# Half-height tiles of TensorE for the block-diagonal products of a fused attention and FFN kernel, and twelve weight pieces split on TensorE

## The chip, the cores and the metric

The kernel runs on one core of a Trainium2 chip. The metric is the device time of one execution in microseconds. The kernel before took 1536.48 us (median of 3 runs, 1536.45 to 1540.12).

## The reference, cut to what matters

Three stages follow each other on 8 batches of 576 tokens with 8 heads of 64 (512 features).

```python
# 1. attention through 32 landmarks (means of 18 tokens)
A, Bm, C = sm(q, k_lm), sm(q_lm, k_lm), sm(q_lm, k)
Z = Bm.T / (norms);  six times: Z = 2 * Z - Z @ Bm @ Z
x = A @ Z @ C @ v                                   # [B, 576, 512] after joining the heads
# 2. Fourier mixing and an FFN of 2048
u = x + real(fft(fft(x, axis=1), axis=2))
un = (u - mean(u)) / sqrt(var(u) + 1e-6)
x = u + relu(un @ w_ch1) @ w_ch2
# 3. a gated FFN of 1024 on token-shifted inputs
k = relu(xk @ w_k);  out = sigmoid(xr @ w_r) * ((k * k) @ w_v)
```

## The kernel before, in words

The 4608 tokens are cut into 9 blocks of 512. Stage 1 and the Fourier part work on one batch at a time, the two FFNs on one block at a time. The large products run in float16 with each operand split into a high and a low half (three products of 128x512 instead of one): 1728 for w_ch1 (named `ph`), 1728 for w_ch2 (`acc`) and 2160 for stage 3. All small products of stage 1 and of the Fourier part are float32 and named `gp`; the profile shows each of those as two MATMUL records, and a transpose as one.

The order is not that of the code. `Plan` records every operation with an estimated cost, then schedules all engines by priority (`Plan.issue`) and issues the instructions of each engine in that order; each engine then works strictly in it. Where the plan believes TensorE idle it adds fillers (`warm`, L1043): products of zeros, into a spare PSUM bank before the first FFN product (`spare<-zero`), later into the open accumulator (`acc<-zero`).

What the change touches, by name and line:

- `Weights.run` (L538): an FFN weight piece of 128x512 arrives in 8-byte words; ACT and DVE make float32 of it (`wst` or `more`), ACT writes the high half (`w1h`, `w2h`), and DVE computes the low half as 64 w - high (`w1l`, `w2l`, L574). Pieces come in the order in which block 0 needs them.
- `series` (L806): after six steps of the inverse, Y (32 landmarks x 64 features for each head, four heads of a group g in 128 partitions) is written as a block diagonal `bdY` of 128x256.
- `tail` (L894): four transposes of `bdY` give `YT`; four products with the table `cs`, each in half of the array's columns (128x64), give the feature side of the Fourier transform (`YC`, `YS`); `mixed(j)` gives the token side of 128 features in `d1`, `d2`, and `xu(t, ...)` multiplies a quarter of the block diagonal by `AT` and adds it to `d1` and `d2` as the next block's input `ub`. There are four `xu` for each batch, each with one product of 289 and one of 288 columns, over all 128 rows of which two heads' rows are zero. The Nyquist row (`psN`, `yn`) is one row of 289 columns.
- `norm(i)` (L1111): for blocks 0 and 1 the mean over features is taken by four products with `ones` and the variance by sixteen one-column products; blocks 2 to 8 add on POOL and DVE first and need one product and four transposes.

```python
for i in range(NB):
    while nb < B and S * nb < BLK * (i + 1):
        batch(nb)
        nb += 1
    block_a(i, norm(i))
```

So block 0 needs batch 0, block 1 needs batch 1, and the other batches are put in between the FFN products of earlier blocks.

Of the kernel before, what the change touches and what calls it, by code (L numbers as in the profile page):

```python
# [11 lines left out]
F32 = mybir.dt.float32  # L12
# [10 lines left out]
M = 32  # L23
# [14 lines left out]
def slot_features():  # L38
    f = np.arange(DM)
    f[257:] = 512 - np.arange(1, 256)  # L40
    return f
# [151 lines left out]
class Plan:  # L193
# [328 lines left out]
class Weights:  # L522
# [15 lines left out]
    def run(self, src, hi, lo, room=None):  # L538
# [35 lines left out]
        v_.scalar_tensor_tensor(lo, w, WS, hi, op0=ALU.mult, op1=ALU.subtract)  # L574
# [4 lines left out]
def phase1(a, iss, psum, const, pool, ident, ublock):  # L579
# [4 lines left out]
    def tile(shape, name, tag=None, bufs=1):  # L584
        return iss.tile(pool, shape, F32, name, tag, bufs)
# [30 lines left out]
    mask4 = load_const("mask4", [128, 4])  # L616
    eye32 = load_const("eye32", [128, M])
# [41 lines left out]
    def chain_a(b):  # L659
# [3 lines left out]
        A = [tile([97, 2, 256], f"A{c}") for c in range(3)]  # L663
# [78 lines left out]
    def chain_b(b):  # L742
# [8 lines left out]
        BB = tile([128, 2, 2, M], "BB")  # L751
# [54 lines left out]
        def series():  # L806
            for i in range(6):
                for g in range(2):
                    ps = psum()[0]
                    w = M + D if i < 5 else D  # L810
                    mm(ps[:, 0:w], flat(bdR[g]), RX[g][:, M + D - w:], True, True)
                    if i < 5:
                        v_.tensor_tensor(bdR[g], spread4(ps[:, 0:M]), m41, op=ALU.mult)
                        s_.activation(RX[g][:, 0:M], ps[:, 0:M], AF.Copy)
                    v_.tensor_tensor(RX[g][:, M:], ps[:, w - D:w], RX[g][:, M:], op=ALU.add)

            bdY = T["bdY", b] = tile([128, 2, 260], "bdY")
            psY = psum()[0]
            for g in range(2):
                mm(psY[:, D * g:D * g + D], flat(bdB[:, g]), RX[g][:, M:], True, True)  # L820
            for g in range(2):
                v_.scalar_tensor_tensor(
                    bdY[:, g, g:g + 256].rearrange("p (h d) -> p h d", d=D),
                    psY[:, D * g:D * g + D].unsqueeze(1).to_broadcast([128, 4, D]),
                    rc[:, g:g + 1], mask4.unsqueeze(2).to_broadcast([128, 4, D]),
                    op0=ALU.mult, op1=ALU.mult,
                )
            g_.tensor_copy(bdY[:, 1, 0:1], bdY[:, 1, 256:257])
# [65 lines left out]
    def tail(b):  # L894
# [9 lines left out]
        YT = tile([128, 2, 2, 64], "YT", "t1")  # L904
        pT = psT.rearrange("p (g x) -> p g x", g=2)
        s_.activation(YT[:, :, 0], pT[:, :, 0:64], AF.Copy)
        s_.activation(YT[:, :, 1], pT[:, :, 192:256], AF.Copy)
# [6 lines left out]
        for g in range(2):  # L914
            ps = psum()[0]
            for hp in range(2):
                mm(
                    ps[64 * hp:64 * hp + 64, :], YT[:, g, hp, :], cs[:, 2 * g + hp, :],
                    True, True,
                )  # L920
            s_.activation(YC[:, g], ps[:, 0:256], AF.Copy)
            s_.activation(YS[:, g, 1:256], ps[:, 257:512], AF.Copy)
            s_.activation(yn[:, g:g + 1], ps[:, 256:257], AF.Copy)
# [3 lines left out]
        def mixed(j):  # L927
# [9 lines left out]
            d1 = tile([128, HS], "d1")  # L937
            d2 = tile([128, HS], "d2")
# [6 lines left out]
            return d1, d2  # L945

        def xu(t, da, db):
            g = t // 2
            pa, pb = psum()[0], psum()[0]
# [4 lines left out]
            for i, lo, hi in cuts(base, base + HS):  # L954
                v_.tensor_tensor(
                    ublock(i)[t][:, lo - BLK * i:hi - BLK * i],
                    pa[:, lo - base:hi - base], da[:, lo - base:hi - base], op=ALU.add,
                )
            end = base + S
            for i, lo, hi in cuts(base + HS, end):  # L960
                l, h = lo - BLK * i, hi - BLK * i
                v_.tensor_tensor(
                    ublock(i)[t][:, h - 1:(l - 1 if l else None):-1],
                    pb[:, end - hi + 1:end - lo + 1], db[:, end - hi + 1:end - lo + 1],
                    op=ALU.add,
                )

        d1, d2 = mixed(0)
        xu(0, d1, d2)
        psN = psum()[0]  # L970
        for g in range(2):
            mm(psN[0:1, 0:HS], yn[:, g:g + 1], AC[:, g], g == 0, g == 1)
        s_.activation(d1[0:1, :], psN[0:1, 0:HS], AF.Copy)
        s_.activation(d2[0:1, :], psN[0:1, 0:HS], AF.Copy)
        xu(2, d2, d1)
        d1, d2 = mixed(1)
        xu(1, d1, d2)
        xu(3, d2, d1)

# [11 lines left out]
def build(nc, tc, a):  # L991
# [5 lines left out]
    with stack, tc.manual_schedule():  # L997
# [50 lines left out]
        iss.warm = warm  # L1048
        w1 = [iss.tile(pa, [128, 4, FF1], F16, f"w1{x}") for x in "hl"]
# [61 lines left out]
        def norm(i):  # L1111
# [4 lines left out]
            if i < 2:  # L1116
# [10 lines left out]
            if i < 2:  # L1127
# [104 lines left out]
        for n, x in enumerate(w12_items):  # L1232
            weights.run(*x, room=rooms[n % 3] if n < 24 else None)
# [169 lines left out]
def consts():  # L1403
    mask2 = np.zeros((128, 2), np.float32)
    mask4 = np.zeros((128, 4), np.float32)
    for p in range(128):
        mask2[p, p // 64] = 1.0 / 18
        mask4[p, p // 32] = 1.0
    eye32 = np.tile(np.eye(M, dtype=np.float32), (4, 1))
# [15 lines left out]
    for i in range(4):  # L1425
        for p in range(128):
            f = 128 * i + p if i < 2 else 511 - (128 * (i - 2) + p)
            ang = 2 * np.pi * ((f * kk) % DM) / DM
            cs[p, i, 0:257] = np.cos(ang)
            cs[p, i, 257:512] = np.sin(ang[1:256])  # L1430
    return dict(
        mask2=mask2, mask4=mask4, eye32=eye32, bones=bones,
# [49 lines left out]
```

## Time and profile before

| | |
|---|---|
| median of the runs | 1536.48 us |
| the profiled execution, whole | 1536.68 us |
| its span, first to last instruction | 1534.9 us |
| TensorE busy | 1522.2 us (99%) |
| VectorE busy | 818.0 us (53%) |
| ScalarE busy | 578.2 us (38%) |
| GpSimd busy | 287.2 us (19%) |
| mean granted TensorE clock | 0.998 |
| first FFN product starts | 77.34 us |

An engine's busy time counts a record from its start to its modelled end; on TensorE records overlap, so the pace is read from the starts, not from the lengths. The interval from one start to the next is what an instruction costs that engine.

### The profile page before, as it was taken

What the parts mean: (1) busy time and instruction counts of PE and PEld (TensorE: products, weight loads), DVE (VectorE), ACT (ScalarE), POOL (GpSimd) and SP (SyncE); (2) the same over time, 40 slices, a digit from 0 to 9 for tenths busy, and PEclk for the clock granted to TensorE, in tenths of its full rate; (3) what the DMA queues carried; (4) which work ended last, traced back from release to release, by engine and by line L of the source; (5) the groups of instructions that cost most, each with busy time, mean ns of one, the idle gap of its engine ahead of it and who ended that gap; (6) DMA issues with size and microseconds to landing.
All of it is one profiled execution on the core that took longest, in us unless ns stands there. A gap on an engine that the chain in (4) does not pass through costs nothing.

```text
span 1534.9 us, 20950 instructions
## 1 busy us (share of the span) xinstructions
PE 1522.2 (99%) x8284; PEld 777.8 (51%) x8284; DVE 818.0 (53%) x1698; ACT 578.2 (38%) x1181; POOL 287.2 (19%) x351
## 2 busy tenths in 40 slices
PE   9999999999999999999999999999999999999998
PEld 5655555555645645645544444444444444444443
DVE  7888667667636426426135171212777765653222
ACT  4667464445413213213212131113655544443221
POOL 3021103113102102102002040001544432231100
PEclk9999999999999999999999999999999999999999
DMA  8434252433301001000004000002011101000000
GB/s 290 159 125 153 79 179 73 144 122 123 101 35 63 32 28 62 2 28 1 1 28 165 1 28 1 28 0 83 28 56 55 55 28 55 28 13 16 28 28 28
DMA packets 43586, 97.86 MB, mean 64 GB/s; under 512 B 4064, under 2 KB 9440, under 8 KB 42976
## 3 DMA queue, kind: packets, MB, share of 16 engines
q1 hardware_dynamic: 43488, 96.53, 18.4%
q8 instruction: 65, 1.06, 0.3%
q14 instruction: 33, 0.27, 0.1%
HBM read 72.39 MB, written 24.12 MB: 63 GB/s over the span
## 4 chain that ended last, share of the span: by engine, by line
PE 96%; DMA 1%; DVE 1%; ACT 1%; issue 0%; SPq 0%; POOL 0%; ACTq 0%; DVEq 0%
PE ph L330 37%; PE acc L330 36%; PE gp L330 21%; PE gp L346 2%; DMA ident<-in_ident 1%; DMA wst<-in_w_ch 0%; DVE small L186 0%; PE spare L1043 0%; SPq L315 0%; DVE uc L186 0%; DMA out<-o 0%; DVE d L186 0%; ACT d L186 0%; ACT wtop L186 0%; DVE o L186 0%
## 5 line engine op out<-in xcount | busy, mean ns | idle before, releaser
L330 PE MATMUL ph<-un,w1h 128*128 128x512 f16 x1152 | 349.9, 379 | 0.4 <-DVE uc L186 0.3
L330 PE MATMUL acc<-h,w2h 128*128 128x512 f16 x1152 | 348.5, 379 | 0.0
L186 DVE SCALAR_TENSOR_TENSOR h<-ph,h 128x512 f16<-128x512 f32 x144 | 99.2, 689 | 302.6 <-ACT h L186 302.2
L186 ACT ACTIVATE h<-ph 128x512 f16<-128x512 f32 x144 | 85.9, 596 | 390.7 <-PE ph L330 390.4
L330 PE MATMUL ph<-un,w1l 128*128 128x512 f16 x576 | 218.6, 380 | 0.0
L330 PE MATMUL acc<-h,w2l 128*128 128x512 f16 x576 | 218.3, 379 | 0.1
L330 PE MATMUL ph<-xk,w_k 128*128 128x512 f16 x864 | 199.6, 379 | 0.0
L330 PE MATMUL acc<-w_v,k 128*128 128x512 f16 x864 | 198.9, 379 | 0.0
L330 PEld LDWEIGHTS <-w2h 128*128 128x128 f16 x1152 | 113.0, 99 | 128.4 <-issue 5.7
L330 PEld LDWEIGHTS <-w1h 128*128 128x128 f16 x1152 | 112.7, 99 | 127.8 <-issue 7.4
L330 PEld LDWEIGHTS <-k 128*128 128x128 f16 x864 | 84.5, 98 | 100.6
L330 PEld LDWEIGHTS <-w_k 128*128 128x128 f16 x864 | 84.5, 98 | 99.7
L186 DVE TENSOR_TENSOR rk<-rk 128x512 f32<-128x512 f32 x72 | 55.5, 770 | 146.3 <-ACT rk L186 145.9
L330 PE MATMUL gp<-w_r,xr 128*128 128x512 f16 x432 | 99.3, 379 | 0.7 <-ACT rs L186 0.7
L186 ACT ACTIVATE rk<-ph 128x512 f32<-128x512 f32 x72 | 42.9, 596 | 129.2 <-PE ph L330 121.6
L330 PEld LDWEIGHTS <-w1l 128*128 128x128 f16 x576 | 57.1, 99 | 65.1 <-issue 4.4
L330 PEld LDWEIGHTS <-w2l 128*128 128x128 f16 x576 | 56.7, 98 | 63.2 <-issue 0.6
L186 DVE TENSOR_TENSOR k<-rk,k 128x512 f16<-128x512 f32 x72 | 59.3, 823 | 29.2 <-ACT k L186 29.0
L186 POOL TENSOR_TENSOR sq<-sq 128x513 f32<-128x513 f32 x27 | 36.7, 1360 | 198.6 <-ACT sq L186 198.1
L186 POOL TENSOR_TENSOR xr<-xt,xr 128x512 f16<-128x512 f32 x36 | 48.6, 1374 | 112.1 <-ACT xr L186 112.0
L330 PEld LDWEIGHTS <-xr 128*128 128x128 f16 x432 | 42.3, 98 | 51.4 <-issue 0.9
L186 DVE TENSOR_TENSOR xt<-xt,rs 128x512 f32<-128x512 f32 x72 | 60.5, 869 | 2.9 <-ACT rs L186 2.8
(162 smaller groups left out, 1919.1 us busy)
## 6 DMA issues: line engine op xcount, KB each, us to landing
wst<-in_w_ch SPq DMA_DIRECT2D x24, 512.0 KB, 3.9
q<-in_q SPq DMA_DIRECT2D x16, 578.0 KB, 5.1
k<-in_k SPq DMA_DIRECT2D x16, 576.0 KB, 4.9
ys<-ub SPq DMA_DIRECT2D x36, 256.0 KB, 2.1
out<-o SPq DMA_DIRECT2D x36, 256.0 KB, 2.1
yb<-ys SPq DMA_DIRECT2D x8, 1026.0 KB, 5.1
v<-in_v SPq DMA_DIRECT2D x8, 1024.0 KB, 5.9
more<-in_w_ch SPq DMA_DIRECT2D x8, 512.0 KB, 4.6
```

The source lines that it names most:

```text
L186: f(real(out), *map(real, args), **{k: real(x) for k, x in kw.items()})
L330: self.nc.tensor.matmul(out.real(), lhsT=lhsT.real(), rhs=rhs.real(), start=start, stop=stop, **kw)
L346: self.nc.tensor.transpose(out.real(), in_.real(), ident.real())
```

## The change

Four things are done.

1. `bdY` holds only two heads side by side (128x128 for a group, was 128x256): rows 0 to 63 are one pair of heads, rows 64 to 127 the other. `xu(g, ...)` issues two products over 64 rows each, into two banks, instead of two over 128 rows. The features are permuted to suit (`slot_features`, `cs`), and `mixed(1)` comes before the first `xu`, with its results in the tiles of `A0` and `A1`.
2. Y is also kept plain (`Y`, an ACT copy), one transpose gives `YT`, and the product with `cs` is eight products in tiles of 64 rows by 32 columns instead of four of 128 by 64.
3. The Nyquist row is computed as two parts of 145 and 144 columns in two column tiles.
4. For the first 12 weight pieces the low half is made by TensorE, 64 w (float32, `scaled`) minus the high half (float16, `minus`) in a PSUM bank, and copied out by ACT; and `norm(1)` goes the way of the later blocks.

```diff
-    def mm(self, out, lhsT, rhs, start, stop, chain=False, **kw):
+    def mm(self, out, lhsT, rhs, start, stop, chain=False, beside=1, **kw):
...
-        op = self.record("pe", run, cost / share, [out], [lhsT, rhs])
+        op = self.record("pe", run, cost / share / beside, [out], [lhsT, rhs])
...
-        v_.scalar_tensor_tensor(lo, w, WS, hi, op0=ALU.mult, op1=ALU.subtract)
+        if subtract:
+            s_.activation(lo, subtract(w, hi), AF.Copy)
+        else:
+            v_.scalar_tensor_tensor(lo, w, WS, hi, op0=ALU.mult, op1=ALU.subtract)
...
-            bdY = T["bdY", b] = tile([128, 2, 260], "bdY")
+            bdY = T["bdY", b] = tile([128, 2, 130], "bdY")
+            Y = T["Y", b] = tile([128, 2, D], "Y")
...
+                s_.activation(Y[:, g], psY[:, D * g:D * g + D], AF.Copy, scale=rc[:, g:g + 1])
...
-        for pr in range(4):
-            g, hp = pr // 2, pr % 2
-            tr(
-                psT[:, 128 * pr:128 * pr + 128],
-                bdY[:, g, g + 128 * hp:g + 128 * hp + 128], ident,
-            )
+        tr(psT[:, 0:128], T["Y", b].rearrange("p g d -> p (g d)"), ident)
...
+        ps2 = psum(2)
+        for h in range(4):
+            for g in range(2):
+                r = slice(64 * g, 64 * g + 64)
                 mm(
-                    ps[64 * hp:64 * hp + 64, :], YT[:, g, hp, :], cs[:, 2 * g + hp, :],
-                    True, True,
+                    ps2[g][M * h:M * h + M, :], YT[r, M * h:M * h + M], cs[r, h, :],
+                    True, True, beside=2, tile_position=(64 * g, M * h),
                 )
...
-            lt = bdY[:, g, 128 * (t % 2):128 * (t % 2) + 128]
-            mm(pa[:, 0:HS], lt, AT[0][:, g], True, True)
-            mm(pb[:, 0:288], lt, AT[1][:, g, 0:288], True, True)
+            rows = [slice(64 * x, 64 * x + 64) for x in range(2)]
+            pa = psum(2)
+            for x, r in enumerate(rows):
+                mm(pa[x][:, 0:HS], bdY[r, g, 0:128], AT[0][r, g], True, True, beside=2)
...
+            pb = psum(2)
+            for x, r in enumerate(rows):
+                mm(pb[x][:, 0:288], bdY[r, g, 0:128], AT[1][r, g, 0:288], True, True, beside=2)
...
-            mm(psN[0:1, 0:HS], yn[:, g:g + 1], AC[:, g], g == 0, g == 1)
+        parts = (0, 0, 145), (32, 145, HS)
+        for g in range(2):
+            for p, lo, hi in parts:
+                mm(
+                    psN[p:p + 1, lo:hi], yn[:, g:g + 1], AC[:, g, lo:hi], g == 0, g == 1,
+                    tile_position=(0, p),
+                )
...
+        def subtract(w, hi):
+            ps = gp()[0]
+            mm(ps, scaled, w, True, False)
+            mm(ps, minus, hi, False, True)
+            return ps
...
-            if i < 2:
+            if i < 1:
...
-            weights.run(*x, room=rooms[n % 3] if n < 24 else None)
+            weights.run(
+                *x, room=rooms[n % 3] if n < 24 else None, subtract=subtract if n < 12 else None
+            )
```

The plan orders everything anew. First place: TensorE in batch 1's `xu`, between FFN products of block 0. Before:

```order
L330 MATMUL gp<-acs,Ao 128x289 x2
L330 LDWEIGHTS w2h
L330 MATMUL acc<-h,w2h 128x512
L330 MATMUL gp<-at,bdY 128x289
L330 LDWEIGHTS w2l
L330 MATMUL acc<-h,w2l 128x512
```

And now:

```order
L333 LDWEIGHTS w2l
L333 MATMUL acc<-h,w2l 128x512
L333 MATMUL gp<-at,bdY 128x289 x2
L333 LDWEIGHTS w2h
L333 MATMUL acc<-h,w2h 128x512
```

The products with `bdY` stand in twos, of 64 rows each; in batches 1 to 7 there are 28 such pairs, and each stands alone between products of the whole array.

Second place: TensorE before the first FFN product of block 0 (`ph`), where `ub,one` and `one,tmp` are block 0's mean and variance and `ident,small` spreads its factors. Before, from the mean on:

```order
L330 MATMUL gp<-ub,one 128x512 x4
L330 MATMUL gp<-ks,qbd 64x32 x4
L346 MATMUL gp<-ident,E 128x128 x4
L330 MATMUL gp<-kbd,q 97x64 x8
L330 MATMUL gp<-one,tmp 128x1 x16
L346 MATMUL gp<-ident,E 128x128
L346 MATMUL gp<-ident,E 64x128
L1043 LDWEIGHTS zero
L1043 MATMUL spare<-zero 128x512
```

And now, from the variance on:

```order
L333 MATMUL gp<-one,tmp 128x1 x16
L333 MATMUL gp<-wst,scaled 128x512
L333 MATMUL gp<-more,scaled 128x512
L333 MATMUL gp<-wst,scaled 128x512
L333 LDWEIGHTS minus
L333 MATMUL gp<-w1h,minus 128x512
L333 LDWEIGHTS minus
L333 MATMUL gp<-w2h,minus 128x512
L349 MATMUL gp<-ident,small 128x128 x4
L333 LDWEIGHTS minus
L333 MATMUL gp<-w1h,minus 128x512
L333 MATMUL gp<-kbd,q 97x64 x5
```

The products of the weight pieces have taken the place of fillers: before the first `ph` there are now ten `scaled`, ten `minus` and 63 fillers (89 before), and batch 1's 40 products `v,ET`, its `BB,c_bones` and its two `et,bdT` have also moved ahead of it. The other two pieces' products stand behind the first `ph`, and no `acc<-zero` is left (13 before).

## Rows read from the trace of the kernel before

**Rows 1.** The page's first part: TensorE busy, share of the span, instructions.
```profile
PE 1522.2 (99%) x8284; PEld 777.8 (51%) x8284; DVE 818.0 (53%) x1698; ACT 578.2 (38%) x1181; POOL 287.2 (19%) x351
```

**Rows 2.** Windows: length, then busy time of each engine, granted clock, DMA.
```profile
40.00:60.00 20.00, 19.06 (x103) 11.41 (x101) 15.15 (x33) 10.95 (x25) 1.71 (x3) 1.00 0.34 110
60.00:77.30 17.30, 17.03 (x100) 10.92 (x98) 15.05 (x42) 13.63 (x30) 0.00 (x0) 0.90 0.64 221
77.30:800.00 722.70, 721.81 (x4373) 395.38 (x4374) 412.97 (x1016) 277.73 (x641) 108.80 (x136) 1.00 0.22 73
```

**Rows 3.** Timeline of TensorE, a batch's transposes and products with the table cs.
```profile
508.51 0.60 PE L346 MATMUL gp<-ident,bdY 128*128 128x128 f32 x4
508.95 0.41 PE L346 MATMUL gp<-ident,A 96*128 96x96 f32 x3
...
509.63 0.38 PE L330 MATMUL ph<-un,w1h 128*128 128x512 f16 x1
509.94 1.95 PE L330 MATMUL gp<-c_cs,YT 128*64 128x512 f32 x8
511.82 0.39 PE L330 MATMUL ph<-un,w1h 128*128 128x512 f16 x1
512.04 0.38 PE L330 MATMUL ph<-un,w1l 128*128 128x512 f16 x1
```

**Rows 4.** Timeline of TensorE, two products with bdY and the Nyquist row.
```profile
795.05 1.14 PE L330 MATMUL gp<-at,bdY 128*128 128x288 f32 x4
796.02 0.59 PE L330 MATMUL ph<-un,w1h 128*128 128x512 f16 x2
...
799.26 0.59 PE L330 MATMUL ph<-un,w1h 128*128 128x512 f16 x2
799.78 1.14 PE L330 MATMUL gp<-acs,yn 128*1 128x289 f32 x4
800.85 0.39 PE L330 MATMUL ph<-un,w1l 128*128 128x512 f16 x1
```

**Rows 5.** Instructions on YT, ET and bdY: least, median and greatest length in ns.
```profile
L330 PEld LDWEIGHTS gp<-c_cs,YT x64: 132/137/137, 40.2 to 739.8; 128*64 128x64 f32 x64
L330 PE MATMUL gp<-c_cs,YT x64: 592/592/644, 40.2 to 740.2; 128*64 128x512 f32 x64
L330 PE MATMUL gp<-v,ET x640: 216/219/244, 20.4 to 722.3; 128*32 128x64 f32 x128, 64*32 64x64 f32 x32
L330 PEld LDWEIGHTS gp<-at,bdY x128: 186/190/201, 45.4 to 811.2; 128*128 128x128 f32 x128
```

**Rows 6.** Timeline of TensorE, block 1's mean and variance.
```profile
169.10 3.64 PE L330 MATMUL gp<-ub,one 128*128 128x512 f32 x8
172.58 0.38 PE L330 MATMUL acc<-h,w2l 128*128 128x512 f16 x1
...
175.39 3.63 PE L330 MATMUL gp<-one,tmp 128*128 128x1 f32 x32
178.88 0.61 PE L330 MATMUL ph<-un,w1h 128*128 128x512 f16 x2
```

**Rows 7.** Windows around the clock's two falls, columns as in Rows 2.
```profile
71.00:73.00 2.00, 2.00 (x7) 0.83 (x6) 1.67 (x11) 1.74 (x5) 0.00 (x0) 0.50 0.44 170
178.00:184.00 6.00, 6.00 (x29) 2.71 (x29) 3.32 (x15) 1.00 (x4) 1.30 (x2) 0.72 0.05 8
```

**Rows 8.** Lines of TensorE by form: the fillers.
```profile
L1043 PE MATMUL spare<-zero 128*128 128x512 f16 x89 | 24.5, 415 | 2.3 <-POOL zero L186 2.3
...
L1043 PE MATMUL acc<-zero 128*128 128x512 f16 x13 | 3.5, 380 | 0.0
```

**Rows 9.** Timeline of TensorE, a batch's products v,ET.
```profile
492.00 1.73 PE L330 MATMUL gp<-v,ET 128*32 128x64 f32 x80
493.66 0.67 PE L330 MATMUL gp<-c_cosT,Ae 96*128 96x289 f16 x4
```

**Rows 10.** Timeline of TensorE, the end of the start-up.
```profile
56.53 0.61 PE L1043 MATMUL spare<-zero 128*128 128x512 f16 x2
...
61.09 3.67 PE L330 MATMUL gp<-ub,one 128*128 128x512 f32 x8
...
74.52 2.57 PE L1043 MATMUL spare<-zero 128*128 128x512 f16 x11
77.34 0.38 PE L330 MATMUL ph<-un,w1h 128*128 128x512 f16 x1 [0.26 <-DVE uc L186]
```

**Rows 11.** Lines of DVE from 33 to 77.3 us: low halves of weight pieces.
```profile
L186 DVE SCALAR_TENSOR_TENSOR w1l<-wst,w1h 128x512 f16<-128x512 f32 x3 | 2.0, 682 | 0.0
```

More of the change, by code (lines that the diff above doesn't have):

```diff
@@ L39, in slot_features @@
     f = np.arange(DM)
-    f[257:] = 512 - np.arange(1, 256)
+    f[257:384] = 512 - np.arange(1, 128)
+    f[385:] = 384 - np.arange(1, 128)
+    f[256], f[384] = 384, 256
     return f
@@ L536, in clear, with run @@
         return x
-    def run(self, src, hi, lo, room=None):
+    def run(self, src, hi, lo, room=None, subtract=None):
         iss = self.iss
@@ L662, in chain_a @@
         q, kbd = T["q", b], T["kbd", b]
-        A = [tile([97, 2, 256], f"A{c}") for c in range(3)]
+        A = [
+            tile([128, 512], f"A{c}")[0:97].rearrange("p (x m) -> p x m", x=2) for c in range(3)
+        ]
         def scores(c):
@@ L750, in chain_b @@
             )
-        BB = tile([128, 2, 2, M], "BB")
+        BB = tile([128, 2, 2, M], "BB", "qs")
         bst = tile([128, 16], "bst")
@@ L897, in tail @@
         psT = psum()[0]
-        for pr in range(4):
-            g, hp = pr // 2, pr % 2
-            tr(
-                psT[:, 128 * pr:128 * pr + 128],
-                bdY[:, g, g + 128 * hp:g + 128 * hp + 128], ident,
-            )
[L904 to L907, printed above, removed]
+        tr(psT[:, 0:128], T["Y", b].rearrange("p g d -> p (g d)"), ident)
+        YT = tile([128, 2, 128], "YT", "t1")[:, 0]
+        s_.activation(YT, psT[:, 0:128], AF.Copy)
         YC, YS = [
@@ L913, in tail @@
         g_.memset(YS[:, :, 0:1], 0.0)
-        for g in range(2):
-            ps = psum()[0]
-            for hp in range(2):
-                mm(
-                    ps[64 * hp:64 * hp + 64, :], YT[:, g, hp, :], cs[:, 2 * g + hp, :],
-                    True, True,
+        ps2 = psum(2)
+        for h in range(4):
+            for g in range(2):
+                r = slice(64 * g, 64 * g + 64)
+                mm(
+                    ps2[g][M * h:M * h + M, :], YT[r, M * h:M * h + M], cs[r, h, :],
+                    True, True, beside=2, tile_position=(64 * g, M * h),
                 )
+        for g, ps in enumerate(ps2):
             s_.activation(YC[:, g], ps[:, 0:256], AF.Copy)
@@ L968, in tail, with xu @@
[L968 to L971, printed above, removed]
-            mm(psN[0:1, 0:HS], yn[:, g:g + 1], AC[:, g], g == 0, g == 1)
[L973 to L978, printed above, removed]
+        def xu(g, ds):
+            rows = [slice(64 * x, 64 * x + 64) for x in range(2)]
+            base = S * b
+            end = base + S
+            pa = psum(2)
+            for x, r in enumerate(rows):
+                mm(pa[x][:, 0:HS], bdY[r, g, 0:128], AT[0][r, g], True, True, beside=2)
+            for x in range(2):
+                for i, lo, hi in cuts(base, base + HS):
+                    v_.tensor_tensor(
+                        ublock(i)[2 * g + x][:, lo - BLK * i:hi - BLK * i],
+                        pa[x][:, lo - base:hi - base], ds[x][0][:, lo - base:hi - base],
+                        op=ALU.add,
+                    )
+            pb = psum(2)
+            for x, r in enumerate(rows):
+                mm(pb[x][:, 0:288], bdY[r, g, 0:128], AT[1][r, g, 0:288], True, True, beside=2)
+            for x in range(2):
+                for i, lo, hi in cuts(base + HS, end):
+                    l, h = lo - BLK * i, hi - BLK * i
+                    v_.tensor_tensor(
+                        ublock(i)[2 * g + x][:, h - 1:(l - 1 if l else None):-1],
+                        pb[x][:, end - hi + 1:end - lo + 1],
+                        ds[x][1][:, end - hi + 1:end - lo + 1], op=ALU.add,
+                    )
@@ new lines, in tail @@
+        d1, d2 = tile([128, HS], "d1"), tile([128, HS], "d2")
+        d3, d4 = [tile([128, 512], n, t)[:, 0:HS] for n, t in (("d3", "A0"), ("d4", "A1"))]
+        mixed(0, d1, d2)
+        mixed(1, d3, d4)
+        xu(0, ((d1, d2), (d3, d4)))
+        s_.activation(d1[0:1, :], d3[0:1, :], AF.Copy)
+        s_.activation(d2[0:1, :], d4[0:1, :], AF.Copy)
+        psN = psum()[0]
+        parts = (0, 0, 145), (32, 145, HS)
[4 more added lines that the diff above has]
+                    tile_position=(0, p),
+                )
@@ L980, in batch @@
+        for d in (d3, d4):
+            for p, lo, hi in parts:
+                s_.activation(d[0:1, lo:hi], psN[p:p + 1, lo:hi], AF.Copy)
+        xu(1, ((d2, d1), (d4, d3)))
     def batch(b):
@@ L1048, in build @@
         iss.warm = warm
+        scaled = iss.tile(p1c, [128, 128], F32, "scaled")
+        minus = iss.tile(p1c, [128, 128], F16, "minus")
+        s_.activation(scaled, ident, AF.Copy, scale=WS)
+        s_.activation(minus, ident, AF.Copy, scale=-1.0)
+        def subtract(w, hi):
[3 more added lines that the diff above has]
+            return ps
         w1 = [iss.tile(pa, [128, 4, FF1], F16, f"w1{x}") for x in "hl"]
@@ L1405, in consts @@
     mask4 = np.zeros((128, 4), np.float32)
+    maskp = np.zeros((128, 2), np.float32)
     for p in range(128):
@@ L1424, in consts @@
     kk = np.arange(257)
-    for i in range(4):
+    for h in range(4):
         for p in range(128):
-            f = 128 * i + p if i < 2 else 511 - (128 * (i - 2) + p)
+            f = D * h + p if p < D else 511 - D * h - (p - D)
             ang = 2 * np.pi * ((f * kk) % DM) / DM
-            cs[p, i, 0:257] = np.cos(ang)
-            cs[p, i, 257:512] = np.sin(ang[1:256])
+            cs[p, h, 0:257] = np.cos(ang)
+            cs[p, h, 257:512] = np.sin(ang[1:256])
     return dict(
-        mask2=mask2, mask4=mask4, eye32=eye32, bones=bones,
+        mask2=mask2, mask4=mask4, maskp=maskp, eye32=eye32, bones=bones,
         ident=np.eye(128, dtype=np.float32),
```

33 lines of the change are left out of this document (9 added, 24 removed).

## The prediction

> **What bounds the kernel now.** I read the page's first part first: TensorE is busy for 1522.2 of 1534.9 us, the next engine for 818 [rows 1]. Then the windows, to see whether that holds stage by stage. From the first FFN product at 77.3 us to 800 us, where batches 1 to 7 lie, TensorE has 0.9 us without a record in 722.7, while DVE is busy for 57% and ACT for 38% [rows 2]. There every instruction taken from TensorE's stream should shorten the run by the interval up to the next start, unless another engine becomes late, and those two have room. Before 77.3 us the picture differs: TensorE looks full too, but 24.5 us of its records in the whole run are fillers, all before the first FFN product [rows 8, 10]. In the start-up TensorE's record share says little; there the end is set by a chain through all engines up to the product at 77.34 us. So I make two sums: the stream after 77.34 us (A), and the start-up (B). Stage 3 is untouched.
>
> **A. The stream after the first FFN product, batches 1 to 7.** All intervals are from start to start.
>
> *Price of a tile mode.* The product with cs runs in 64-column tiles. The FFN product ahead of it starts at 509.63 and would cost 0.216 (as the one from 511.82 to 512.04), yet cs starts at 509.94: 0.09 us to enter. Its eight records, two side by side, take 1.88 us to the next FFN product [rows 3]; four turns of 0.43 (a 128x512 float32 record, 3.48 / 8 [rows 6]) would be 1.72. So 0.16 more, of which 0.05 is a longer first record (644 against 592 ns), the rest leaving the mode. For 32-column weights the first record is 0.025 longer (244 against 219) [rows 5]. Hence some 0.26 us for a stay in 64 columns, 0.24 in 32.
>
> *xu.* Two products with bdY take 0.97 us now [rows 4], a product 0.485. Side by side they need 0.485 and a stay in a mode, which here loads weights of 128 columns; their load takes 190 ns against 137 for 64 [rows 5], so I add 0.05: 0.31. A pair 0.80, saved 0.17 on each of 28 pairs: -4.8. No row shows two tiles of 64 rows side by side (rows 5 have 64x32 tiles in one half of the rows only); column tiles do overlap fully. From both sides: -6.2 if the larger weights cost nothing more, +8.7 (28 x 0.31) if the two run one after the other. I take the overlap, as the column tiles are the nearest row.
>
> The Trainium skill, page "TensorE: Matmul & The Clock Gate", section "Measured speedup vs the span model", has four row tiles at 3.07 times the pace of one, so 77% of full overlap. By that the pair would take 0.94 instead of 0.80, the 28 pairs would save 0.8 us instead of 4.8, and the forecast below would be 4 us later; no run here shows it, and the column tiles of this trace overlap better.
>
> *cs.* Now 0.09 + 1.88 = 1.97. Eight products side by side: 0.86 for the two records, 0.24 for the mode, and some 0.1 for eight starts instead of two (an estimate; the ends are 0 and 0.2): 1.20. Saved 0.77, times 7: -5.4. If the two row halves take turns, the gain is nil.
>
> *Nyquist row.* 0.09 to enter and 1.07 for four records of 0.243 and the way out [rows 4]: 1.16. With half the columns in two tiles 0.49 of work and the same mode: 0.68. -0.48 times 7: -3.4.
>
> *Transposes.* Four take 0.44 [rows 3]; three go: -0.33 times 7: -2.3.
>
> *Block 1's norm.* The mean takes 3.48 us and becomes one product (0.87), the sixteen one-column products take 3.49 [rows 6] and become four transposes (0.44): -5.7. Right behind those one-column products the granted clock fell to its lower level: 0.72 over the 6 us from 178 [rows 7], which is 28% of 6: 1.7 us lost. With them gone I expect no fall: -1.7. POOL and DVE get the sums instead, in a stretch where both have room.
>
> *Fillers.* 13 acc<-zero go, 0.216 each: -2.8. They stood in a full stream.
>
> *Added.* Two of the twelve pieces lie here: 0.87 + 0.22 each: +2.2.
>
> *Moved ahead.* 40 products v,ET (1.66 us and a mode, 1.75 [rows 9]) and the few bones and et products (0.6, six records by the pace of transposes): -2.4, which B gets.
>
> Sum of A: -4.8 - 5.4 - 3.4 - 2.3 - 5.7 - 1.7 - 2.8 + 2.2 - 2.4 = -26.3.
>
> **B. The start-up.** Ten pieces are put into TensorE's stream ahead of the first FFN product: 10 x 1.09 = +10.9. Moved in from A: +2.4. Batch 0's own savings: transposes 0.33, cs 0.77, Nyquist 0.48, and of its eight products with bdY two pairs (0.35) and one run of four (1.94 to 1.28): -2.6. Fillers: 26 fewer, 0.216 each: -5.6. If TensorE waits as long as now besides, the first FFN product comes 5.1 later. What speaks for less: DVE is busy for 87% from 60 us on [rows 2] and loses the low halves, 0.68 each [rows 11], about seven of them by 77 us: 4.8. What speaks for more: the fillers removed stood in real waits, partly before the mean (56.5 to 61 us) and partly before the end (74.5 to 77.3) [rows 10], and TensorE takes its instructions in order: each scaled waits for DVE's word, each minus for ACT's high half, and behind them stand the mean and the variance of block 0. And the clock falls from some 70 us on, at 0.50 from 71 to 73 us [rows 7], now under fillers, afterwards under the pieces' products: up to 1.7. So from 0 to +12.4 (5.1 + 5.6 + 1.7); I take +5.
>
> The ACT copies (one for each piece, in place of DVE's instruction) cost nothing in the sum: ACT is busy for 79% from 60 to 77 us, DVE for 87% [rows 2]. If that cover is gone, ten copies of about 0.6 would each hold up the un halves, up to 6 us; this lies within the bound.
>
> **Sum.** -26.3 + 5 = -21.3 on the profiled execution's 1536.68 us, which is 0.2 above the median: 1515.2 against it, and I say 1515. With the start-up at its ends: 1510 and 1523. With xu's ends too: from 1509 to 1536.
>
> **Rivals.**
> 1. *The halves take turns.* Tiles of 64 rows don't overlap, though four column tiles of one half do. xu +8.7 instead of -4.8, cs 0 instead of -5.4, and batch 0 loses some 2.5 more: 1515 + 13.5 + 5.4 + 2.5 = 1536, no change. For it: no row shows an overlap of row halves. Against it: the column tiles' eight records stand two by two.
> 2. *Slower: the halves exclude each other, and cs pays.* Its eight products alternate between upper and lower rows, so if a change of half lets nothing overlap, all eight stand one after the other: 8 x 0.86 + 0.24 = 7.1 us instead of 1.97. Against the forecast that is 5.9 more in each of 8 batches, 47 us, beside rival 1's 16: 1578. It decides the sign from 4.6 us for a batch's eight (1.97 + 21.3 / 8). Against it: the four column tiles of v,ET run at 21 ns a record [rows 9], although they too read different data.
> 3. *The start-up eats the gain.* The pieces' products wait in order for ACT and DVE, and the mean, the variance and the first FFN product behind them: 10 waits of 1 us on top of the 5: 1525. For it: the in-order queue, and three scaled and two minus right between variance and spread. Against it: DVE is relieved.
> 4. *Another engine becomes late* in A, because batches 1 to 7 have less time. Half the gain of A: 1528. Against it: 57% and 38%.
>
> **Chances.** Forecast with its bounds 0.75, rival 1 0.06, rival 2 0.04, rival 3 0.08, rival 4 0.04, better than 1507 0.03. The range 1507 to 1526 leaves out rivals 1, 2 and 4 and some of 3. A measurement tells a change of 0.3% (4.6 us) from none. Faster: 0.75 + 0.08 + 0.04 + 0.03 = 0.90; rival 1 sits in the middle of no change: 0.05 with what lies near; slower 0.05.
>
> **What would show it.** Right: pairs at-bdY with both first records within a few ns and 0.80 us to the next product; cs with eight records started together and 1.2 us; yn 0.68; no clock fall near 180 us; the first FFN product near 82 us, and no more idle TensorE after it than now. Wrong: second halves starting after the first ones' end; idle time of TensorE ended by ACT (w1h, w2h) or DVE (wst) ahead of the mean; a first FFN product later than 90 us, or gaps between 82 and 800 us.

## The result and the profile after

The changed kernel takes 1521.91 us (median of 4 runs, 1521.46 to 1522.47), the kernel before 1537.92 (4 runs, 1536.45 to 1540.12) on the same chip: ratio 0.9895, 95% interval 0.9878 to 0.9912. The change is faster by about 1%. Its profiled execution took 1522.28 us (span 1520.0), 14.4 less than the one before, where 21.3 less was forecast: the direction holds and the time lies in the range, but a third of the gain is missing.

The page's first part, as [rows 1]:

```profile
PE 1503.9 (99%) x8319; PEld 755.7 (50%) x8319; DVE 805.9 (53%) x1688; ACT 597.5 (39%) x1235; POOL 291.7 (19%) x355
```

Windows of the changed kernel, columns as in [rows 2]:

```profile
60.00:80.00 20.00, 20.00 (x176) 13.88 (x175) 16.10 (x46) 16.32 (x33) 2.71 (x3) 0.91 0.43 150
80.00:100.00 20.00, 15.73 (x81) 8.93 (x75) 16.31 (x49) 15.63 (x37) 4.77 (x6) 0.88 0.66 217
95.10:101.90 6.80, 6.63 (x21) 3.99 (x22) 4.53 (x15) 3.77 (x11) 2.20 (x3) 0.50 0.26 78
...
200.00:800.00 600.00, 597.95 (x3763) 319.06 (x3762) 322.40 (x809) 214.36 (x523) 89.34 (x112) 1.00 0.19 62
```

The second of these windows in the kernel before:

```profile
80.00:100.00 20.00, 20.00 (x171) 10.38 (x170) 17.62 (x47) 11.82 (x24) 5.39 (x6) 1.00 0.55 176
```

Before, TensorE had a record nearly all the time from 77.3 to 800 us. Now it is without one for 4.3 of the 20 us from 80 to 100; 6.8 us, from 95.1 us on, run at the lower clock; and 2 us are missing between 200 and 800. The busy shares do not explain the gaps by themselves: DVE is busy for 82% of that window, but it was for 88% before, when TensorE had no gap; ACT has risen from 59% to 78%.

Timeline of TensorE, the new forms and the stretch behind the first FFN product, answering to [rows 3, 4, 10]; the brackets hold idle time and what ended it:

```profile
41.19 1.09 PE L333 MATMUL gp<-c_cs,YT 64*32 64x512 f32 x16
42.21 1.17 PE L333 MATMUL gp<-more,scaled 128*128 128x512 f32 x2
...
50.81 0.66 PE L333 MATMUL gp<-acs,yn 128*1 128x145 f32 x8
51.40 2.15 PE L333 MATMUL gp<-k,qbd 128*64 128x288 f32 x14
53.48 0.76 PE L333 MATMUL gp<-at,bdY 64*128 64x289 f32 x4
54.17 0.70 PE L333 MATMUL gp<-k,qbd 128*64 128x288 f32 x2
...
80.47 0.59 PE L333 MATMUL ph<-un,w1h 128*128 128x512 f16 x2
...
85.09 0.38 PE L333 MATMUL gp<-w1h,minus 128*128 128x512 f16 x1 [0.96 <-ACT w1h L188]
85.84 1.17 PE L333 MATMUL gp<-more,scaled 128*128 128x512 f32 x2 [0.38 <-DVE more L188]
...
92.58 0.46 PE L333 MATMUL gp<-RX,bdR 128*128 128x96 f32 x2 [1.87 <-ACT RX L188]
...
95.27 0.72 PE L333 MATMUL gp<-RX,bdR 128*128 128x96 f32 x2 [1.06 <-DVE RX L188]
95.78 1.06 PE L333 MATMUL acc<-h,w2h 128*128 128x512 f16 x2
...
298.83 0.38 PE L333 MATMUL ph<-un,w1l 128*128 128x512 f16 x1
299.68 1.53 PE L333 MATMUL gp<-c_sinT,Ao 96*128 96x289 f16 x11 [0.47 <-DVE bdY L188]
```

Eight cs products (16 records) take 1.02 us to the next start, where [rows 3] had 1.88 for four. A pair with bdY takes 0.69 and with the 0.09 of its entry 0.78; two took 0.97 [rows 4]. The Nyquist row takes 0.59, with the entry 0.68. The four bracketed waits stand within 11 us, and at 95.78 two acc records take 1.06 instead of the 0.59 of the two at 80.47. The last line is a wait that the batch's products with c_sinT did not have before.

Lines of the tiles YT and bdY, columns as in [rows 5]:

```profile
L333 PEld LDWEIGHTS gp<-c_cs,YT x128: 102/104/106, 41.2 to 738.1; 64*32 64x32 f32 x128
L333 PE MATMUL gp<-c_cs,YT x128: 589/601/613, 41.2 to 738.6; 64*32 64x512 f32 x128
L333 PEld LDWEIGHTS gp<-at,bdY x128: 182/186/187, 49.3 to 801.5; 64*128 64x128 f32 x128
L333 PE MATMUL gp<-at,bdY x128: 400/403/508, 49.3 to 801.8; 64*128 64x289 f32 x64, 64*128 64x288 f32 x64
```

A record of cs is hardly longer than in [rows 5] (601 against 592 ns) although it shares the array with more tiles: twice as many records run in about half the time.

The timelines of TensorE also give where each block's FFN begins. The table has the start of its first ph product in us, in the changed kernel and in experiments told below:

| | block 0 | 1 | 2 | 3 | 4 | 5 | 6 | 7 | span |
|---|---|---|---|---|---|---|---|---|---|
| before | 77.3 | 207.1 | 339.2 | 453.6 | 568.7 | 683.8 | 793.8 | 887.3 | 1534.9 |
| after | 80.5 | 205.4 | 332.6 | 444.2 | 557.2 | 670.1 | 782.1 | 872.6 | 1520.0 |
| e1, no pieces | 77.8 | 195.9 | 328.9 | 441.0 | 553.9 | 666.9 | 778.8 | 869.3 | 1516.8 |
| e4, one reader of Y's bank | 80.1 | 201.3 | 328.0 | 439.5 | 551.8 | 664.1 | 775.5 | 866.0 | 1513.4 |
| e10, no pieces, one reader | 78.0 | 197.1 | 329.2 | 441.1 | 553.4 | 665.8 | 777.1 | 867.6 | 1515.1 |
| e5, e10 without fillers | 78.4 | 200.3 | 332.3 | 444.3 | 556.6 | 668.9 | 780.2 | 870.7 | 1518.2 |

Differences of a row's neighbours are the lengths of blocks. Against before, the changed kernel starts 3.1 later, gains 4.9 and 4.8 in blocks 0 and 1 (the sum A had put about 15 there: 26.3 less 5 batches of 2.27), and 8.2 in blocks 2 to 6 (11.3 in the sum). These two parts are not quite separate, because the plan also shifts small products across block borders (24 products `kbd,q` of 3.4 us into blocks 2 to 6, four products of 2.0 us with `acs` out of them). Blocks 3 and 4 hold the same work before and after but for the new forms: each is 2.2 shorter, where 2.27 was forecast. From block 7 on nothing changes.

### The profile page after: what moved, and what is told of

Same layout as the page of the kernel before. It is cut to its first block, busy times and chain, and to the rows that moved or that the text cites. A ratio compares the mean times of both kernels' runs of the same rounds, so it can differ in the third digit from the quotient of the medians.

```text
span 1520.0 us, 21083 instructions
## 1 busy us (share of the span) xinstructions
PE 1503.9 (99%) x8319; PEld 755.7 (50%) x8319; DVE 805.9 (53%) x1688; ACT 597.5 (39%) x1235; POOL 291.7 (19%) x355
## 4 chain that ended last, share of the span: by engine, by line
PE 97%; DVE 1%; ACT 1%; DMA 0%; issue 0%; POOL 0%; DVEq 0%; ACTq 0%; POOLq 0%
PE acc L333 37%; PE ph L333 37%; PE gp L333 21%; PE gp L349 2%; PE spare L1062 1%; DVE small L188 0%; DMA wst<-in_w_ch 0%; DVE bdY L188 0%; ACT Y L188 0%; DMA out<-o 0%; ACT E L188 0%; DVE cst L188 0%; DVE o L188 0%; DVE bdR L188 0%; ACT ET L188 0%
```

## The experiments

Two theories at first. One: the terms of the tiles are right, and the missing 7 us lie in the waits that the pieces leave behind the first FFN product, in the clock's fall there, and in the waits ahead of c_sinT. The other: the row tiles overlap less than their records suggest, and the gain comes from elsewhere. Each ratio below is against the kernel before, run beside it on the same chip (medians 1538.69 us for e1 to e4, 1536.79 for e5 to e8, 1538.70 for e9 to e11), so runs of different groups are compared by their ratios.

**The norm alone**, on the kernel before:

```diff
-            if i < 2:
+            if i < 1:
```

> The kernel before with only block 1's norm by POOL and DVE sums, one product and four transposes. Prediction's terms: -5.7 us of products, -1.7 us as the clock's fall near 180 us goes with the one-column products, +2.8 for 13 more acc<-zero in the plan: about 1533 us and no half-rate stretch near 180 us. Rival (the fall has another cause): the stretch stays and 1534.5 us or more.

1533.78 us, ratio 0.9976 (0.9965 to 0.9986). The window of [rows 7]'s second line, in this kernel:

```profile
178.00:184.00 6.00, 6.00 (x34) 2.85 (x32) 5.15 (x17) 3.27 (x10) 2.51 (x3) 1.00 0.48 165
```

The granted clock is 1.00 where it was 0.72: no fall follows when the sixteen one-column products are gone. Of the 5.7 + 1.7 us of the two terms only some 3.7 arrive (0.24% of 1537) when the edit stands alone; in the profiled executions it is 2.8 (1533.88 against 1536.68). The products themselves do what was forecast: from start to start those of the norm take 5.7 us less in blocks 0 and 1. But this plan puts 26 acc<-zero there instead of 13, which take 3.4 us more.

**The row tiles without the pieces** (the changed kernel with `subtract` never given):

```diff
-    subtract=subtract if n < 12 else None
+    subtract=subtract if n < 0 else None
```

> The changed kernel without the weight pieces on TensorE (all low halves by DVE, as before); the half-height tiles, the one transpose, the parted Nyquist row and block 1's norm stay. Theory P (the pieces cost the missing 8 us: they wait in TensorE's in-order stream behind the first FFN product, batch 1's series waits behind ACT, and the clock falls after it): the four gaps between 83 and 96 us (5.1 us) and the clock's fall at 95 to 102 us (3.4 us) are gone; the plan puts 26 acc<-zero fillers in (2.8 us more than before's 13); the whole about 1513 us, first FFN product near 77 us. Rival R (the new order of the half-height tiles makes the gaps by itself): gaps and fall stay, 1521 us or more.

1519.54, ratio 0.9881 (0.9866 to 0.9895): about 2.4 us less than the changed kernel, but the intervals overlap, so that the two are not told apart. Its windows from 77.5 to 200 and from 200 to 800 us:

```profile
77.50:200.00 122.50, 121.94 (x734) 64.20 (x734) 92.09 (x212) 76.94 (x156) 23.07 (x27) 1.00 0.38 130
200.00:800.00 600.00, 597.35 (x3768) 319.52 (x3765) 327.51 (x819) 217.36 (x532) 91.67 (x119) 1.00 0.19 62
```

The waits behind the first FFN product and the clock's fall are gone with the pieces, as the first theory said, but the time follows by only a third: this plan puts 26 acc<-zero fillers (6.7 us) into blocks 0 and 1. The table shows it: block 0 is 6.8 us shorter than in the changed kernel, block 1 5.8 longer. The waits ahead of c_sinT stay (2.65 us without a record in the second line); they do not come from the pieces. Nor does the edit take out the pieces alone: with them gone, the plan puts batch 1's products `v,ET` back behind the first FFN product.

**The pieces without the row tiles**, on the kernel before:

```diff
+        if subtract:
+            s_.activation(lo, subtract(w, hi), AF.Copy)
+        else:
             v_.scalar_tensor_tensor(lo, w, WS, hi, op0=ALU.mult, op1=ALU.subtract)
```

> The kernel before with only the twelve pieces' low halves by TensorE and an ACT copy (cp in A2's place, to make room); tiles, norm and transposes as before. Theory P: the first FFN product some 3 us later, and 6 to 8 us lost behind it in gaps and a half-rate stretch, less 2.8 for the 13 acc<-zero that the plan no longer adds: 1543 to 1547 us, slower than before. Rival R (the pieces fill time in which TensorE only had fillers, and cost nothing): 1535 to 1539 us.

The edit also gives `cp` the place of `A2`, to make room; what that costs was not run by itself.

1546.19, ratio 1.0052 (1.0035 to 1.0070): slower. Its first FFN product stands at 83.7 us (77.3 before), and waits follow, though for other tiles than in the changed kernel (ET, un and wst, none for RX):

```profile
87.00:99.00 12.00, 10.55 (x121) 5.82 (x119) 10.74 (x32) 10.23 (x24) 2.54 (x3) 1.00 0.62 196
```

TensorE is without a record for 1.45 of 12 us, with DVE at 90% and ACT at 85%, and the clock does not fall there. The waits are not where most of the time goes: of the 9.2 us between the profiled executions (1545.93 against 1536.68) 6.4 are the later start, ahead of which the clock is at its lower level for 6.8 us instead of 3.4; blocks 0 and 1 together are only 0.9 longer. By themselves the pieces cost time in this kernel, and mainly in the start-up, which theory P had at 3 us.

**One reader of Y's bank.** In the changed kernel ACT copies Y out of PSUM and DVE builds bdY from the same bank. ACT and DVE at this step of the changed kernel, ahead of the wait shown above:

```profile
298.19 0.31 ACT L188 ACTIVATE Y<-gp,bst 128x64 f32<-128x64 f32 x1 [3.19 <-PE gp L333]
298.54 0.35 DVE L188 SCALAR_TENSOR_TENSOR bdY<-gp,bst,c_maskp 128x128 f32<-128x128 f32 x1 [1.23 <-ACT Y L188]
298.93 0.31 ACT L188 ACTIVATE Y<-gp,bst 128x64 f32<-128x64 f32 x1 [0.42 <-DVE bdY L188]
...
299.27 0.35 DVE L188 SCALAR_TENSOR_TENSOR bdY<-gp,bst,c_maskp 128x128 f32<-128x128 f32 x1 [0.38 <-ACT Y L188]
```

Each waits for the other, in turns, and the bank is held for 1.43 us. The Trainium skill, page "PSUM — Partial Sum Buffer", section "PSUM bank collisions raise a hardware error", says that accesses of two different engines to one bank collide when they fall on the same quadrant of 32 partitions at the same moment, a ScalarE read with a VectorE read included. No run here shows a collision; the releasers in these rows show that this program keeps the two readers apart. The edit lets DVE read Y from SBUF:

```diff
             for g in range(2):
                 s_.activation(Y[:, g], psY[:, D * g:D * g + D], AF.Copy, scale=rc[:, g:g + 1])
-                v_.scalar_tensor_tensor(
+            for g in range(2):
+                v_.tensor_tensor(
                     bdY[:, g, g:g + 128].rearrange("p (h d) -> p h d", d=D),
-                    psY[:, D * g:D * g + D].unsqueeze(1).to_broadcast([128, 2, D]),
...
+                    Y[:, g].unsqueeze(1).to_broadcast([128, 2, D]),
```

> The changed kernel, but bdY is made from the plain Y in SBUF instead of from PSUM, so only the two ACT copies hold the bank of Y's product. Theory B (the waits of 0.3 to 0.6 us before c_sinT,Ao in five batches come from that bank, which the ACT copies and DVE's block diagonals hold in turns for 1.4 us): the waits are gone, 2.9 us less, about 1519 us. Rival (the wait is for something else, and the bank is only the last named): the waits stay and the time stays within 1 us of 1522.

1516.64, ratio 0.9862 (0.9847 to 0.9877), the lowest of this study; the interval ends just below that of the changed kernel. ACT, DVE and TensorE's c_sinT at the same step:

```profile
294.15 0.52 ACT L188 ACTIVATE Y<-gp,bst 128x64 f32<-128x64 f32 x2 [3.39 <-PE gp L333]
294.50 0.50 DVE L188 TENSOR_TENSOR bdY<-Y,c_maskp 128x128 f32<-128x128 f32 x2 [1.38 <-ACT Y L188]
294.95 1.28 PE L333 MATMUL gp<-c_sinT,Ao 96*128 96x289 f16 x9
```

The bank is free after 0.52 us. Windows:

```profile
95.00:102.00 7.00, 6.86 (x45) 4.60 (x43) 6.35 (x21) 4.11 (x15) 1.81 (x3) 1.00 0.26 76
200.00:800.00 600.00, 600.00 (x3699) 318.78 (x3699) 322.51 (x804) 213.27 (x519) 92.70 (x116) 1.00 0.19 62
```

No wait is left between 200 and 800 us: theory B holds for the waits ahead of c_sinT, and blocks 3, 4 and 5 are each 0.6 us shorter. In this execution the clock does not fall at 95 us either. The four waits that stood there in the changed kernel (0.96, 0.38, 1.87 and 1.06 us by the brackets above) are still there (total, times, longest):

```profile
PE gp L333 <- ACT RX L188: 1.3, 1, 1.3
PE gp L333 <- DVE RX L188: 1.1, 1, 1.1
PE gp L333 <- ACT w1h L188: 1.0, 1, 1.0
PE gp L333 <- DVE more L188: 0.4, 1, 0.4
```

One is 0.56 us shorter, 1.31 for 1.87. ACT shows why, in the changed kernel and then in this one:

```profile
90.67 0.67 ACT L188 ACTIVATE wst<-wst 128x512 f32<-128x512 int8 x1 [0.96 <-DMA wst<-in_w_ch]
```

```profile
89.78 0.66 ACT L188 ACTIVATE wst<-wst 128x512 f32<-128x512 int8 x1 [0.39 <-DMA wst<-in_w_ch]
```

ACT stands idle for the words of a weight piece, and its copy of RX comes behind that piece in its order (after `wst`, `h` and `wtop`, at 92.34 and 91.45 us). The words were issued at 85.06 us and taken up 5.6 us later in the changed kernel, at 84.73 and 5.05 later here; TensorE and ACT do the same things in the same order between. So the wait of 1.87 us was in part one for a transfer, and that it is shorter here is not shown to come from the edit. Nor is the clock's better course: two of the four executions of this kernel take 1515.6 us at a mean clock of 0.998 (the profiled one among them) and two 1517.6 or 1517.7 at 0.997, while all four of the changed kernel have 0.996. What the rows give the edit is 2.9 us; what else lies between the two ratios, 0.9895 and 0.9862, is open.

**Without pieces and with one reader**, with the fillers and without them:

```diff
-    subtract=subtract if n < 12 else None
+    subtract=subtract if n < 0 else None
...
-                        if m == 3 and f == 0 and n == 0:
-                            op.opens = acc[3]
-                        if m == 3 and f == 15 and n == 1:
-                            op.closes = True
```

(the first hunk alone is e10, both are e5, each on top of e4)

> As the run without pieces and fillers, with the plan's 30 acc<-zero fillers. Theory C (they fill real waits in blocks 0 and 1 and keep the clock from falling): no half-rate stretch between 80 and 1500 us, block 2 starts at 328 to 330 us, 1515 to 1517 us, faster than the same without fillers (1520). Rival F (they lengthen the stream, 30 x 0.216): 1522 us or more.

> The half-height tiles, the one transpose and block 1's norm, no weight pieces on TensorE, bdY made from Y in SBUF, and no acc<-zero fillers (the plan would put 30 in). From the run without pieces (1518.9 us profiled): the 26 fillers cost 0.216 each, -5.6; the waits before c_sinT go, -3.5: about 1510 us, faster than the changed kernel. Theory F (the fillers only lengthen a full stream): no clock fall appears behind the first FFN product. Rival C (they hold the clock up): one to three half-rate stretches of 3.4 us, 1.7 us each, 1511.5 to 1515.

e10: 1517.38, ratio 0.9868 (0.9855 to 0.9882). e5: 1520.18, 0.9891 (0.9876 to 0.9906). The window behind the first FFN product, e10 and then e5, and what TensorE waited for in e5 from 77 to 205 us:

```profile
77.50:200.00 122.50, 121.55 (x734) 63.75 (x734) 91.61 (x211) 76.35 (x155) 22.50 (x27) 1.00 0.40 128
```

```profile
77.50:200.00 122.50, 117.64 (x689) 61.16 (x690) 88.35 (x205) 76.22 (x156) 23.17 (x26) 0.96 0.39 124
...
165.50:172.30 6.80, 5.84 (x12) 2.18 (x13) 5.99 (x11) 3.58 (x6) 0.97 (x1) 0.50 0.24 80
```

```profile
PE ph L333 <- DVE w1l L188: 2.2, 1, 2.2
PE gp L333 <- DVE A L188: 1.4, 2, 1.1
PE acc L333 <- DVE w2l L188: 1.3, 1, 1.3
...
```

Taking the 30 fillers out (30 x 0.216 = 6.5 us) shortens nothing: TensorE waits for DVE's low halves instead, and from 165.5 us on, inside the wait of 2.2 us that begins at 164.27, the clock is at 0.50 for 6.8 us. The theory that these fillers only lengthen the stream, which gave about 1510 for e5 and 1522 or more for e10, is refuted. e10 came out near theory C: no low stretch behind the first FFN product, and block 2 at 329.2 us. That the kernel with them is faster is likely and no more: the two intervals overlap a little.

**The same on the kernel before**: only the second hunk.

> The kernel before without its 13 acc<-zero fillers, nothing else. Theory F: 13 x 0.216 = 2.8 us less, 1534 us against 1537, no more half-rate stretches than before. Rival C: further clock falls, 1.7 us each, so 1535.5 us or more.

1538.05, ratio 1.0005 (0.9997 to 1.0014). The stretch of [rows 7]'s second fall, here:

```profile
178.00:186.00 8.00, 8.00 (x33) 4.08 (x33) 2.82 (x15) 1.35 (x5) 1.30 (x2) 0.57 0.19 60
```

Taking out the 13 acc<-zero changes nothing that the runs can tell. In this execution TensorE is without a record for 2.0 us from 77.5 to 200 us, where the kernel before had almost none, and the low stretch is 6.8 us long instead of 3.4; on the other hand the fall of [rows 7]'s first line, in the start-up, is missing here. So most of the fillers stood in place of waits.

**Full rows.** e5 with the products of bdY over all 128 rows and zeros in between, one after the other as before:

```diff
-                mm(pa[x][:, 0:HS], bdY[r, g, 0:128], AT[0][r, g], True, True, beside=2)
+                mm(pa[x][:, 0:HS], bdY[:, g, x, 0:128], AT[0][:, g], True, True)
```

> As the run without pieces, with bdY from Y and without fillers, but the products with bdY use all 128 rows (two block diagonals with the other half's rows zero, one after the other), in the same pairs and banks. This leaves the half-height tiles of that product alone as the difference. Theory T (halves overlap, a stay in their mode costs some 0.3 us): a pair takes 0.97 us instead of 0.79, 28 pairs and batch 0's four: 5 to 6.5 us slower than the kernel with half-height tiles. Rival (the mode's price eats the overlap): within 1 us.

DVE also writes four block diagonals for two here. 1519.41, ratio 0.9893 (0.9879 to 0.9906), as long as e5. Its records:

```profile
L333 PE MATMUL gp<-at,bdY x128: 403/407/511, 45.3 to 801.3; 128*128 128x289 f32 x64, 128*128 128x288 f32 x64
```

From their start to the next start these take 27.23 us behind the first FFN product, in e5 20.29. Of these 6.9 us the entries into the mode take 2.6 back (28 of 0.09), so the tiles save 4.3 us of TensorE, and blocks 3 to 5 are each 0.7 shorter with them. Yet the sums agree, since e5 loses in blocks 0 and 1 what it gains later: its block 3 begins at 444.3, that of e8 at 443.5. Much of that loss is the clock's: in e5 it is at 0.50 for 10.2 us there (165.5 to 172.3 and 196.3 to 199.7), in e8 for 3.4, which is 3.4 us of time. (The profiled execution of e8 took 1521.21; it is the longest of its four.) This is the miss in small: a true saving, eaten by waits and the clock in the first two blocks.

**Fewer pieces on TensorE**, 10 and 8 instead of 12, with one reader:

```diff
-    subtract=subtract if n < 12 else None
+    subtract=subtract if n < 10 else None
```

> As the run with bdY from Y in SBUF, with ten weight pieces on TensorE instead of twelve: the order up to the first FFN product is the same, and only the two pieces behind it go back to DVE (three acc<-zero are planned). Theory S (the two pieces wait in order for ACT's high half and DVE's word, 1.1 and 0.5 us, beside their 2.2 us of products): the gaps at 83 to 86 us go, block 1 starts 3 to 4 us earlier than in the run with twelve, 1512.5 to 1514 us. Rival L (the stretch is bound by the weights' own chain on ACT and DVE, and TensorE's waits only move): within 1 us of it, 1516 us, with waits of the same sum further on.

> The changed kernel with bdY from Y in SBUF and only eight weight pieces on TensorE, all of which stand ahead of the first FFN product; no acc<-zero is planned. Theory Q (the pieces' harm is their place in the in-order stream behind the first FFN product): no waits of over 0.5 us between 80 and 100 us, no half-rate stretch there, the first FFN product at 79 to 81 us, 1510 to 1512 us. Rival W (any piece on TensorE costs its 1.1 us wherever it stands, as the start-up is bound by TensorE too): first FFN product at 83 us or more, 1514 us or more.

With 10: 1518.01, ratio 0.9873 (0.9859 to 0.9886). With 8: 1519.75, 0.9894 (0.9880 to 0.9907). The run with 8 decides neither Q nor W: its plan puts 112 spare fillers in (63 with 12 pieces), and 50 of them run in one row from 76.75 to 87.9 us, ahead of the first FFN product at 89.4, though DVE has the last half of `un` ready at 81.3. As far as the rows show, fillers and not pieces hold TensorE for most of the delay here. What TensorE waited for from 77 to 110 us with 10 pieces:

```profile
PE ph L333 <- DVE RX L188: 4.9, 1, 4.9
PE gp L333 <- DVE RX L188: 1.4, 2, 1.3
PE acc L333 <- DVE RX L188: 0.7, 1, 0.7
```

The waits of the pieces (w1h, more) are gone and the one for RX has grown to 4.9: with its low halves back, DVE is what all wait for. The waits move, and their sum is 7.0 us where it was 3.8 with twelve pieces, so rival L is nearer than theory S; S's earlier start of block 1 is there too, at 199.3 for 201.3 us, but the time is no shorter.

**The low halves' copy on DVE**, on e4:

```diff
-            s_.activation(lo, subtract(w, hi), AF.Copy)
+            v_.tensor_copy(lo, subtract(w, hi))
```

> As the run with bdY from Y in SBUF, twelve pieces on TensorE, but their low halves copied from PSUM by DVE instead of ACT. Theory A (behind the first FFN product TensorE waits for an ACT that the copies made late: the wait of some 1.5 to 2 us for RX by ACT): that wait is under 0.5 us. Rival O (the wait comes from the order of batch 1's series right behind the first FFN product, whoever copies): 1 us or more stays. The time in either case between 1513 and 1520 us, as DVE then has its old load and TensorE the pieces too.

1525.84, ratio 0.9924 (0.9911 to 0.9938): slower. The first FFN product comes at 90.1 us, and the wait is DVE's now:

```profile
PE gp L333 <- DVE RX L188: 3.7, 3, 2.1
...
```

The wait for RX by ACT is gone, as theory A had it, and more than 1 us of waiting for RX stays, as rival O had it. DVE writes RX too, so moving the copies to DVE only moved the load, and the run does not tell whether they delay RX. The plan also put 24 more fillers ahead of the first FFN product (87 for 63).

**What goes with the waits for RX.** RX holds the steps of batch 1's inverse: TensorE multiplies, ACT and DVE write RX, and TensorE multiplies again. TensorE's products of these steps from 77 to 115 us, before and in the changed kernel:

```profile
L330 PE MATMUL gp<-RX,bdR x24: 219/275/275, 93.2 to 111.3; 128*128 128x96 f32 x20, 128*128 128x64 f32 x4
```

```profile
L333 PE MATMUL gp<-RX,bdR x24: 219/275/530, 88.4 to 102.7; 128*128 128x96 f32 x20, 128*128 128x64 f32 x4
```

They began 15.9 us behind the first FFN product and took 18 us; now they begin 7.9 behind it and take 14, waits included. The plan could place them so because batch 1's products `v,ET` had moved ahead of the first FFN product. In all five kernels where they did (the changed one, e4, e6, e9, e11) TensorE waits for RX between 77 and 110 us; of the eight others only e8 has such a wait, one of 1.5. No run changed this order alone, so it remains an argument.

## Why the prediction was right in its direction and 7 us off

- **xu, cs, Nyquist, transposes (15.9 of the sum's 26.3): right.** A pair 0.78 for 0.80, cs 1.11 (0.09 + 1.02) for 1.20, yn 0.68 for 0.68. Blocks 3 and 4, which hold the same work otherwise, gain 2.2 each and with Y's bank freed 2.8, where 2.27 was forecast; over blocks 2 to 6 it is 8.2 and 10.2 for 11.3, with other products shifted across their borders. Rivals 1 and 2 (halves in turns or excluding each other) are refuted by the records and by e8. The 0.94 that follows from the Trainium skill's 3.07 ("TensorE: Matmul & The Clock Gate", "Measured speedup vs the span model") is not what two tiles of 64 float32 rows do here: the measurement decides, and it is nearly full overlap.
- **Block 1's norm and the clock near 180 us: right in kind.** The fall at 179 us is gone in every kernel with the edit (e5 and e8, without fillers, have others at 165 to 172 or 195 to 200). The products' 5.7 us are there in e3; alone the edit gives 2.8 to 3.7 of 7.4, as the plan adds 3.4 us of fillers.
- **The step that failed: "There every instruction taken from TensorE's stream should shorten the run", applied from the first FFN product on, blocks 0 and 1 included.** It rested on one window of 722.7 us [rows 2] and on busy shares, "those two have room". A share did not tell: from 80 to 100 us DVE was busy for 88% before without a gap, and for 82% after with 4.3 us of gaps. As far as the rows show, what counted was the order, in which TensorE reached products before their inputs were there. Its freed time became waits for RX and pieces (4.4 us by the rows) and 3.4 us lost to the lower clock that came with them in the traced execution. The prediction had also booked the products "Moved ahead" as 2.4 from A to B and nothing else; with them batch 1's steps came 8 us closer to the first FFN product. By its own signs ("gaps between 82 and 800 us") this part was wrong.
- **13 fillers, -2.8: wrong.** They looked like full stream because a filler has a record. e7 puts their price at nothing (ratio 1.0005), and e10 against e5 (0.9868 and 0.9891, with intervals that overlap a little) has the kernel with 30 of them rather faster. Not all fillers are free: in e6 a row of 50 holds up the first FFN product.
- **Not in the sum at all: the second reader of Y's bank.** The prediction gave the added ACT copy of Y no price. It was not ACT's time that counted but the bank's: DVE's bdY came later and c_sinT waited 0.63 in four batches and 0.35 in a fifth, by the timeline, 2.9 us in all. Removing it gives 1516.64, and 1515.66 in the profiled execution against a forecast of 1515.2. That e4 lands so near is partly luck: 2.9 us are the bank's, the clock's 3.4 are not shown to be, and the waits of 83 to 96 us, which the sum did not have, remain and are offset by terms that came out better than forecast (2.8 for 2.27 in blocks 3 and 4, the start-up).
- **Start-up, +5: +3.1 measured**, with the first FFN product at 80.5 for 82 us. Rival 3's mechanism (pieces waiting in order for ACT and DVE) is there, but in the changed kernel mostly behind that product: 1.0 for w1h, 0.4 for more. Without the tiles (e2) the pieces move the start by 6.4.
- **Rival 4 (another engine late in A)** had 4%, on shares averaged over 7 batches. In kind it is what happened, in the first two blocks, and c_sinT's waits are of its kind too. The time lies in the range because the range, 1507 to 1526, was wide.

What the pieces on TensorE are worth: alone +7.5 us (e2, with the move of `cp`), with the row tiles about +2.4 that the intervals do not tell from nothing (after against e1), with one reader nothing that can be measured (e4 and e10). It is open what sets the end of blocks 0 and 1 in e4: every variant moved the waits between RX, pieces and fillers, and none showed them shorter without a cost elsewhere.

## What to carry to other kernels

Read the waits stage by stage before adding up a stream's savings: where the stream holds fillers it only looks full, and the busy shares of the other engines do not tell whether an input will be ready when its product's turn comes. A second engine that reads a PSUM tile had a price here even with time to spare, namely the time it added until the bank was free (1.43 us for 0.52); copying once to SBUF and letting the other read there removed it. Where two 64-row halves of the array have independent work, put it side by side.

## What was not expected of the hardware

- Eight 64x32 tiles run abreast: 16 records of 0.60 us each (median 601 ns) in 1.02 us, a record hardly longer than with two tiles (592 ns [rows 5]).
- A half-height float32 tile costs no more load than a full one (186 against 190 ns), and 32 columns load in 104 where 64 took 137.
- In one execution a wait of 1.87 us and one of 1.06 behind it were followed by 6.8 us at a granted clock of 0.50; in one of e4, 1.31 and 1.05 in the same place were followed by none.
